# Top-k attention and a GELU layer on one core: reciprocals of the softmax sums made by POOL as a power, and eight more odd items transposed by DVE and DRAM

## The chip, the core and the metric

The program runs on one core of a Trainium2 chip. A core has five engines, each with a queue of its own that runs in the order in which the program was written: PE (TensorE: matmuls and transposes into PSUM), DVE (VectorE), ACT (ScalarE), POOL (GpSimd) and SP (SyncE, which here issues nearly all DMAs). They wait for each other through semaphores. Work that one queue holds up behind a wait stays held up, however ready it is.

The metric is the device time of one execution in microseconds (us); lower is better. The kernel before takes 1462.1 us, the median of three runs that lie between 1461.39 and 1462.64 us.

## The reference

Two blocks follow each other. The first is attention that keeps the 32 largest scores of each row:

```python
B, H, S, D = 8, 8, 576, 64
scores = (1 / sqrt(D)) * q @ k.transpose(0, 1, 3, 2)          # B, H, 576, 576
kth    = the 32nd largest of each row
scores = where(scores >= kth, scores, -1e9) - max of the row
attn   = exp(scores)
attn   = attn / (attn.sum(-1, keepdims=True) + 1e-09)
x      = (attn @ v).transpose(0, 2, 1, 3).reshape(B * S, H * D)   # 4608 x 512
```

The second is a layer with an exact GELU, `out = gelu(x @ w_in) @ w_out`, with `w_in` 512 x 2048 and `w_out` 2048 x 512. Everything is float32.

## The kernel before

**Items.** Heads are taken in pairs. An item is 128 rows of the scores of one pair: a tile `s` of 128 partitions by 2 x 576 scores (one row of each of the two heads in a partition). Each head has 576 = 4 x 128 + 64 rows. For each batch there are 16 items of full row blocks (4 pairs x 4 blocks, two neighbouring blocks of a pair after each other) and 2 items that hold the 64 remaining rows of two pairs each. That makes 18 items a batch and 144 in all. Two batches, 36 items, are one ring of the buffer of x, and the pattern repeats with that period: an item's *number in the period* is its index modulo 36. Numbers 16 to 19 are the items of remaining rows; apart from those, two neighbouring numbers (even, odd) share one product with v.

**Slots.** The main loop runs over slots n. In slot n the engines work on different items:

- PE multiplies q and k for items ahead (L408, L423: `s_ps`, and L373: `t_ps`, the last keys); from slot 14 on an even slot does it for two items, n+2 and n+3. ACT copies the scores to `s` (L416, L381).
- DVE runs `top_k(n)`: rounds of MAX8 and MATCH_REPLACE8 (L513, L516) that find the 32nd largest. Most items are "paired": `larger` (L446, DVE) makes the elementwise maximum of the two halves of each row, `sum_up` (L477) and `smaller` (L485) on POOL make the minimum, so that the first two rounds read half the elements.
- POOL makes the threshold of item n (`threshold`, L527 and L528). ACT selects and exponentiates item n-1 (L547, L559); the exponential also sums the row into `den`.
- POOL adds 1e-9 to `den` of item n-1 (`add_small`, L540), DVE takes the reciprocal (`inverse`, L534, in `last()` at the end of `top_k(n)`), and POOL multiplies the item by it (`normalise`, L582).
- Item n-2 has to be transposed, since the product with v contracts over the keys. There are two ways. *By PE:* `transposes` gives 1 + 8 PE transposes of 128 x 128 into PSUM (L666, L680), and ACT copies the result to `pt` (L669, L695). *Squared:* DVE transposes 32 x 32 squares in place (`square_p`, L614, in the middle of `top_k(n)`), SP writes the item to DRAM with four DMAs (`write_p`, L624, at the end of slot n), and a slot later SP reads it back in the wanted order with four DMAs (`read_p`, L634). For a squared item PE and ACT do neither the transposes nor the copies.
- PE multiplies `pt` by v (`attend`, L751, L762). This is done once for an even and an odd item together: 20 matmul records. `pt` has one buffer, so that the read of the next even item waits for this product.
- PE fills the rest of the slot with pieces of the GELU layer (`mlp`; L820 first matrix, L976 and L974 second one, with a seven-product scheme). `room_in(n)` says how many pieces a slot gets. What is left after the last item is done at the end.

**Which items are squared.** `squared(i)`: from item 27 on, every even item but number 12, the items of remaining rows but number 17, and the odd items that `moved(i)` names, those of 36 to 135 whose number is in `LATER = (3, 13, 25, 31)`. The product of a moved odd item is done in slot i+4, not i+3, in the middle of that slot (`mid`, `mids`). In such a slot `read_p(n - 3)` is issued only behind that product, followed by loads of v that were held back (`issue_soon`); `bare(n)` in `room_in` moves two GELU pieces between the neighbouring slots to make up for it.

**SP's queue.** The DMAs of one slot stand in this order: `read_p(n-3)` (where no product is pending), loads of q and k that follow the DVE transposes of the slot (L130), in a `mid` slot `read_p(n-3)` here, then held loads of v (L140, L144), `write_p(n-2)`, and stores of the output (L891).

Of the kernel before, what the change touches and what calls it, by code (L numbers as in the profile page):

```python
# [14 lines left out]
def kernel(  # L15
# [19 lines left out]
    nc = tc.nc  # L35
    f32, i32, u32 = mybir.dt.float32, mybir.dt.int32, mybir.dt.uint32
    bf16, i16, u16 = mybir.dt.bfloat16, mybir.dt.int16, mybir.dt.uint16
    AF = mybir.ActivationFunctionType
    ALU = mybir.AluOpType

    B, H, S, D = q.shape
    P = 128
# [19 lines left out]
    const = ctx.enter_context(tc.tile_pool(name="const", bufs=1))  # L62
# [47 lines left out]
    def flush():  # L110
        held[0] = False
        while late_issues:
            late_issues.pop(0)()
        late_issues.extend(later)
        later.clear()
# [61 lines left out]
    DIAGS = START - 1  # L177
    SINGLE = range(18, 28)
    words = {}
    bounds = const.tile([P, 2], f32, name="bounds")  # L180
    low, high = bounds[:, 0:1], bounds[:, 1:2]
    nc.gpsimd.memset(low, -EXP0 * 2.0**20)
    nc.gpsimd.memset(high, EXP0 * 2.0**-40)

# [71 lines left out]
    for b in range(B):  # L258
# [4 lines left out]
        last = [(b * NP + p, NM) for p in range(0, NP, 2)]  # L263
# [8 lines left out]
    N = len(items)  # L272
# [4 lines left out]
    few = [False]  # L277
# [55 lines left out]
    S_of, stat_of = {}, {}  # L333
# [98 lines left out]
    def paired(i):  # L432

        return PAIRED <= i < N and i not in SINGLE

    def halves_of(i):
        s = S_of[i].rearrange("p (e h n) -> p e h n", e=2, h=2)
        return s[:, :, 0], s[:, :, 1]

    have_larger = set()  # L440

    def larger(i):

        if paired(i) and i not in have_larger:
            have_larger.add(i)
            nc.vector.tensor_tensor(lists_for(i)[:, :, 0], *halves_of(i), op=ALU.max)  # L446

    def into_of(i):

        if i < 2 and i not in into_lists:  # L450
            into_lists[i] = work.tile([P, 2, 2, HS], f32, tag="pt", bufs=1, name="into")
        return into_lists.get(i, lists_of[i])
# [13 lines left out]
    def lists_for(i):  # L466

        if i not in lists_of:
            lists_of[i] = work.tile([P, 2, 2, HS], f32, tag="lists", name="lists")
        return lists_of[i]  # L470
# [10 lines left out]
    def smaller(i):  # L481

        if paired(i):
            both, top = lists_of[i][:, :, 1].bitcast(i32), lists_of[i][:, :, 0].bitcast(i32)
            nc.gpsimd.tensor_tensor(into_of(i)[:, :, 1].bitcast(i32), both, top, op=ALU.subtract)  # L485

    def top_k(i, last, middle):


        stat_of[i] = st = {  # L490
            "first": work.tile([P, 2, 8], f32, tag="first", name="first"),
        }
        stat = work.tile([P, 4, 2], f32, tag="stat", name="stat")
        st.update((n, stat[:, x]) for x, n in enumerate(("neg", "bias", "den", "rden")))
        top = work.tile([P, 2, 16], f32, tag="top", bufs=1, name="top")
        into = [st["first"]] + [
            top[:, :, 8:16] if r == TOPK // 8 - 1 else top[:, :, 0:8] for r in range(1, TOPK // 8)
        ]
        if paired(i):
            t = lists_of[i]  # L500
            u = into_of(i)
            both = u.rearrange("p e h n -> p e (h n)")
            rounds = [(t[:, :, 0], u[:, :, 0]), (u[:, :, 0], u[:, :, 0])]
            rounds = [(*(rounds[r] if 16 * r < TOPK else (both, both)), x) for r, x in enumerate(into)]
        else:
            s = S_of[i].rearrange("p (e n) -> p e n", e=2)
            t = work.tile([P, 2, S], f32, tag="lists", name="rest")
            rounds = [(s if r == 0 else t, t, x) for r, x in enumerate(into)]
        for r, (src, dst, x) in enumerate(rounds):
            if 16 * r == TOPK:  # L510
                middle()
            for e in range(2):
                nc.vector.max(x[:, e], src[:, e])  # L513
            if r < len(rounds) - 1:
                for e in range(2):
                    nc.vector.match_replace(dst[:, e], x[:, e], src[:, e], LOWEST)  # L516
            if r == len(rounds) - 1:
                last()

        st["kth"] = top[:, :, 15]  # L520

    def threshold(i):

        if i < 0 or i >= N:
            return
        st = stat_of[i]
        nc.gpsimd.tensor_scalar(st["neg"], st["kth"], -1.0, None, op0=ALU.mult)  # L527
        nc.gpsimd.tensor_tensor(st["bias"], st["kth"], st["first"][:, :, 0], op=ALU.subtract)  # L528

    def inverse(i):  # L530
        if i < 0 or i >= N:
            return
        st = stat_of[i]
        nc.vector.reciprocal(st["rden"], st["den"])  # L534

    def add_small(i):
        if i < 0 or i >= N:
            return
        st = stat_of[i]
        nc.gpsimd.tensor_scalar(st["den"], st["den"], 1e-9, None, op0=ALU.add)  # L540

    def select(i, e):

        if i < 0 or i >= N:
            return
        st, s = stat_of[i], row(i, e)
        nc.scalar.activation(s, s, func=AF.Prelu, bias=st["neg"][:, e : e + 1], scale=1.0, alpha=STEEP)  # L547
        selected.add((i, e))
# [37 lines left out]
    def squared(i):  # L586

        if not SINGLE.stop - 2 < i < N - 2:
            return False
        if items[i][1] == NM:  # L590
            return i % RINGS != RINGS // 2 - 1
        return moved(i) or (i % 2 == 0 and i % RINGS != 12)

    LATER = (3, 13, 25, 31)

    def moved(i):

        return RINGS <= i < N - 8 and i % RINGS in LATER

# [10 lines left out]
    def square_p(i):  # L610

        if squared(i):
            s = S_of[i]
            nc.vector.transpose(s, s)  # L614

    def write_p(i):

        if squared(i):
            turned[i] = d = dram.tile([SQ, NJ + NM, P // SQ, P], f32, tag="turned", name="turned")
            s = S_of.pop(i).rearrange("p (x j) -> p x j", j=SQ)  # L620
            d = d.rearrange("i c k n -> i (c k) n")
            for a in range(P // SQ):
                rows = slice(a * SQ, (a + 1) * SQ)
                nc.sync.dma_start(out=d[:, :, rows], in_=s[rows])  # L624
# [498 lines left out]
    def mlp(n):  # L1123
        for _ in range(n):
            if done[0] >= len(pieces) or pieces[done[0]][0] > ready[0] or left[0] == 0:
                return
            pieces[done[0]][1]()
            done[0] += 1
            left[0] -= 1
            if eager[0]:  # L1130
                run_gelus()
                run_small(9)
# [72 lines left out]
    for n in range(ahead):  # L1205
# [27 lines left out]
        if n > 0:  # L1233
            larger(n + 1)
# [58 lines left out]
        if few[0]:  # L1293
            room = ODD if n % 2 else 0
            if mid and (mid[0] in starts_next or mid[0] % RINGS == LATER[0]):
                mlp(1)
# [34 lines left out]
            softmax(n - 1, 1)  # L1331
        if n > 0:
            smaller(n + 1)
        add_small(n - 1)
        for piece in tr[-1:] + prep:
            piece(None)
            mlp(1)
# [5 lines left out]
        mlp(left[0])  # L1343
        run_gelus()
        if n < N:
            def last():
                if few[0]:
                    larger(n + 2)
                inverse(n - 1)

            top_k(n, last, lambda: square_p(n - 2))
            write_p(n - 2)
            flush()
            if n == 0:
                larger(1)
        else:
            inverse(n - 1)
        threshold(n)
        if n == 0:
            smaller(1)  # L1360
# [60 lines left out]
```

## Time and profile before

| | |
|---|---|
| median of 3 runs | 1462.1 us |
| the profiled execution's own time | 1461.3 us |
| its span, first to last instruction | 1459.5 us |
| granted TensorE clock | 1.00 |
| busy in the span: PE, DVE, ACT, POOL | 1442.6, 1329.6, 1056.4, 1128.4 us |
| last top-k ends, GELU pieces alone follow | about 1375 us |
| items transposed by DVE and DRAM | 68 of 144 |

Busy time is the time in which an engine had an instruction in work; the start of a matmul record to the start of the next is the pace of PE. In the groups, the columns are the line, the engine, the operation, the output and inputs with their shapes and the count; behind the first bar stand the busy time in us and the mean length of one in ns, behind the second the idle time of the engine just before them and what ended most of it. In a timeline the columns are the start in us, the length in us and the instructions, equal neighbours merged with their count. SP's DMA rows show the issue, and not the transfer.

### The profile page before, as it was taken

How to read it: one execution, taken by the hardware profiler on the slowest of the kernel's cores; microseconds unless marked ns; L12 is line 12 of the kernel's file. 1: busy time of each engine (PE TensorE's matmuls, PEld its weight loads, DVE VectorE, ACT ScalarE, POOL GpSimd, SP SyncE). 2: the span in 40 equal slices, each digit the busy share in tenths (PEclk: the TensorE clock that was granted, in tenths of full speed). 3: DMA queues.
4: the chain of work that ended last, by engine and by line, in shares of the span. 5: the costliest groups of instructions: out<-in, count | busy, mean ns of one | idle time of the engine just before them, and what ended most of it. 6: DMA issues, size and time to landing. Idle time of an engine off the chain costs nothing.

```text
span 1459.5 us, 26550 instructions
## 1 busy us (share of the span) xinstructions
PE 1442.6 (99%) x8621; PEld 1123.9 (77%) x8621; DVE 1329.6 (91%) x3339; ACT 1056.4 (72%) x1883; POOL 1128.4 (77%) x1290
## 2 busy tenths in 40 slices
PE   8999999999999999999999999999999999999999
PEld 6776678877777777787777778787777777787887
DVE  7999999999999999999999999999999999999601
ACT  7999977777777777767777777777676767677620
POOL 6877657877798878878888878887788887878632
PEclk9999999999999999999999999999999999999999
DMA  7524310045454446456554365456554444543200
GB/s 196 150 87 126 84 48 1 9 98 104 90 113 89 87 87 142 82 113 128 111 99 96 65 117 116 90 112 127 117 102 106 90 80 84 127 98 85 53 15 15
DMA packets 591819, 136.49 MB, mean 94 GB/s; under 512 B 504352, under 2 KB 583232, under 8 KB 591680
## 3 DMA queue, kind: packets, MB, share of 16 engines
q1 hardware_dynamic: 590416, 134.37, 43.5%
q8 instruction: 68, 1.11, 0.3%
q14 instruction: 71, 0.58, 0.1%
q10 hardware_dynamic: 1200, 0.39, 0.1%
q0 software_dynamic: 64, 0.03, 0.0%
HBM read 85.19 MB, written 49.55 MB: 92 GB/s over the span
## 4 chain that ended last, share of the span: by engine, by line
PE 44%; POOL 11%; DVE 7%; issue 3%; ACT 3%; DMA 1%; SPq 0%; DVEq 0%; POOLq 0%; ACTq 0%
PE h_ps L820 17%; PE y_ps L976 11%; PE o L751 5%; PE s_ps L408 3%; POOL s L582 3%; DVE top L513 3%; DVE lists L516 2%; POOL lists L485 2%; POOL lists L477 2%; PE seven L974 2%; PE tp L680 2%; PE y_ps L938 2%; PE y_ps L941 1%; DMA turned<-s 1%; DVE s L614 1%
## 5 line engine op out<-in xcount | busy, mean ns | idle before, releaser
L820 PE MATMUL h_ps<-xT,w_in_sb 128*128 128x256 f32 (+1 forms) x2560 | 533.0, 361 | 0.0
L820 PEld LDWEIGHTS h_ps<-xT,w_in_sb 128*128 128x128 f32 x2560 | 438.9, 191 | 69.2 <-issue 10.9
L513 DVE MAX8 top<-lists 128x8 f32<-128x576 f32 (+1 forms) x792 | 475.9, 641 | 0.0
L547 ACT ACTIVATE s<-s,stat 128x576 f32<-128x576 f32 x288 | 219.2, 786 | 123.0 <-POOL stat L527 122.9
L516 DVE MATCH_REPLACE8 lists<-top,lists 128x288 f32<-128x288 f32 (+1 forms) x528 | 308.0, 589 | 0.0
L582 POOL TENSOR_TENSOR s<-s,stat 128x1152 f32<-128x1152 f32 x135 | 284.8, 2109 | 10.1 <-DVE stat L534 5.3
L559 ACT ACTIVATE s<-s,stat 128x576 f32<-128x576 f32 x288 | 225.2, 787 | 7.6
L485 POOL TENSOR_TENSOR lists<-lists 128x576 int32<-128x576 int32 x132 | 186.6, 1413 | 3.1
L477 POOL TENSOR_TENSOR lists<-s 128x576 int32<-128x576 int32 x133 | 188.2, 1415 | 0.0
L540 POOL TENSOR_SCALAR stat<-stat 128x2 f32<-128x2 f32 x144 | 44.4, 309 | 163.0 <-ACT s L559 156.1
L751 PE MATMUL o<-pt,raw_v 128*64 128x256 f32 x1280 | 152.9, 384 | 1.0 <-ACT pt L685 0.4
L416 ACT ACTIVATE s<-s_ps 128x1024 f32<-128x1024 f32 x127 | 126.4, 1046 | 35.2 <-PE s_ps L408 35.0
L751 PEld LDWEIGHTS o<-pt,raw_v 128*64 128x64 f32 x1280 | 86.8, 136 | 80.9 <-issue 38.1
L976 PE MATMUL y_ps<-w_out_sb,sum 128*128 128x256 f32 x472 | 140.4, 379 | 0.0
L408 PE MATMUL s_ps<-kt,qm 64*128 64x512 f32 x512 | 131.2, 621 | 1.1 <-ACT s L414 0.8
L836 ACT ACTIVATE g<-h_ps 128x512 f32<-128x512 f32 x144 | 78.2, 595 | 66.6 <-PE h_ps L820 66.0
L446 DVE TENSOR_TENSOR lists<-s 128x576 f32<-128x576 f32 x133 | 106.2, 799 | 17.8 <-ACT s L381 5.8
L976 PE MATMUL y_ps<-w_out_sb,g 128*128 128x256 f32 x480 | 116.4, 382 | 0.0
L516 DVE MATCH_REPLACE8 lists<-first,lists 128x288 f32<-128x288 f32 x264 | 114.4, 439 | 0.0
L513 DVE MAX8 first<-lists 128x8 f32<-128x288 f32 x268 | 105.8, 434 | 0.0
L976 PEld LDWEIGHTS y_ps<-w_out_sb,g 128*128 128x128 f32 x480 | 90.4, 190 | 15.0 <-issue 3.1
L976 PEld LDWEIGHTS y_ps<-w_out_sb,sum 128*128 128x128 f32 x472 | 89.8, 190 | 12.1
(162 smaller groups left out, 2359.0 us busy)
## 6 DMA issues: line engine op xcount, KB each, us to landing
turned<-s SPq DMA_DIRECT2D x272, 144.0 KB, 3.6
pt<-turned SPq DMA_DIRECT2D x272, 144.0 KB, 3.2
raw_v<-in_v_dram SPq DMA_DIRECT2D x64, 128.0 KB, 2.5
raw_q<-in_q_dram SPq DMA_DIRECT2D x112, 72.0 KB, 2.3
raw_k<-in_k_dram SPq DMA_DIRECT2D x112, 72.0 KB, 2.4
out_dram<-y SPq DMA_DIRECT2D x30, 256.0 KB, 3.1
w_out_sb<-in_moe_w_in_dram SPq DMA_DIRECT2D x14, 511.8 KB, 4.9
w_out_sb<-in_moe_w_out_dram SPq DMA_DIRECT2D x10, 511.8 KB, 4.1
```

The source lines that it names most:

```text
L408: nc.tensor.matmul(s_ps[:, e], lhsT=q_t[rows, :], rhs=kt[rows, main_keys(pair)], start=True, stop=True)
L416: nc.scalar.activation(spread(s, S + TL, SM), s_ps, func=AF.Copy, scale=scale)
L477: nc.gpsimd.tensor_tensor(t[:, :, 1].bitcast(i32), a.bitcast(i32), b.bitcast(i32), op=ALU.add)
L485: nc.gpsimd.tensor_tensor(into_of(i)[:, :, 1].bitcast(i32), both, top, op=ALU.subtract)
L513: nc.vector.max(x[:, e], src[:, e])
L516: nc.vector.match_replace(dst[:, e], x[:, e], src[:, e], LOWEST)
L547: nc.scalar.activation(s, s, func=AF.Prelu, bias=st["neg"][:, e : e + 1], scale=1.0, alpha=STEEP)
L559: nc.scalar.activation(s, s, func=AF.Exp, bias=st["bias"][:, e : e + 1], scale=1.0, accum_out=st["den"][:, e : e + 1],)
L582: nc.gpsimd.tensor_tensor(s, s, wide, op=ALU.mult)
L751: nc.tensor.matmul(o[e * D : (e + 1) * D, 0:n], lhsT=vt[:, j, e, :], rhs=pt[:, e * NJ + j if j < NM else NM, :], start=(j == 0), stop=(j = ...
L820: nc.tensor.matmul(h_tile(u)[:, i, :], lhsT=w_in_sb[:, ko, f * P : (f + 1) * P], rhs=xT[:, ko, c0 : c0 + n], start=(ko == 0), stop=(ko == ...
L976: nc.tensor.matmul(acc[names][:, k], lhsT=lhsT, rhs=rhs, start=(j == 0 and k == 0), stop=(j == FT // 2 - 1 and k == 1),)
```

## The change

Two things are changed. The reciprocal of `den` is no longer made by DVE: POOL does it right behind its addition of 1e-9, as `den` to the power of -1, with the exponent in a third column of `bounds`. The hook at the end of `top_k` goes away with it, so that `larger(n + 2)` is written at the start of slot n+1 and not at the end of slot n. And `LATER` has three more numbers, 5, 23 and 33. In the range that `moved` allows these are the items 41, 77, 113, 59, 95, 131, 69 and 105: they are transposed by DVE and DRAM, and their product with v comes a slot later.

```diff
-    bounds = const.tile([P, 2], f32, name="bounds")
+    bounds = const.tile([P, 3], f32, name="bounds")
+    minus = bounds[:, 2:3]
...
+    nc.gpsimd.memset(minus, -1.0)
...
-    def top_k(i, last, middle):
+    def top_k(i, middle):
...
-            if r == len(rounds) - 1:
-                last()
...
     def inverse(i):
...
-        nc.vector.reciprocal(st["rden"], st["den"])
-
-    def add_small(i):
...
         nc.gpsimd.tensor_scalar(st["den"], st["den"], 1e-9, None, op0=ALU.add)
+        nc.gpsimd.tensor_tensor(
+            st["rden"], st["den"],
+            bass.AP(tensor=minus.tensor, offset=minus.offset, ap=[list(minus.ap[0]), [0, 2]]),
+            op=ALU.pow,
+        )
...
-    LATER = (3, 13, 25, 31)
+    LATER = (3, 5, 13, 23, 25, 31, 33)
...
-        add_small(n - 1)
+        inverse(n - 1)
...
         if n < N:
-            def last():
-                if few[0]:
-                    larger(n + 2)
-                inverse(n - 1)
-
-            top_k(n, last, lambda: square_p(n - 2))
+            top_k(n, lambda: square_p(n - 2))
...
-        else:
-            inverse(n - 1)
```

`larger` loses the set that kept it from running twice for an item. In the order of the engines' instructions the change takes 144 reciprocals from DVE and gives it 8 square transposes; POOL gets 144 powers; PE loses 8 x (1 + 8) transposes and ACT 8 x 2 copies from PSUM; SP gets 8 x (4 + 4) DMAs. Three of the pairwise maxima change places with a neighbour on DVE.

More of the change, by code (lines that the diff above doesn't have):

```diff
@@ L438, in halves_of @@
         return s[:, :, 0], s[:, :, 1]
-    have_larger = set()
     def larger(i):
-        if paired(i) and i not in have_larger:
-            have_larger.add(i)
+        if paired(i):
             nc.vector.tensor_tensor(lists_for(i)[:, :, 0], *halves_of(i), op=ALU.max)
@@ L533, in inverse @@
         st = stat_of[i]
-        nc.vector.reciprocal(st["rden"], st["den"])
-    def add_small(i):
[L537 to L540, printed above, removed]
+        nc.gpsimd.tensor_scalar(st["den"], st["den"], 1e-9, None, op0=ALU.add)
+        nc.gpsimd.tensor_tensor(
[3 more added lines that the diff above has]
+        )
     def select(i, e):
```

## The prediction

> **What bounds the kernel now.** I read the busy line of the page, the stages of the span, the timelines of PE and SP, and the waits. In a stage, the columns are its length, then busy time of PE, PE's weight loads, DVE, ACT and POOL, the clock, and the DMA share.
>
> ```profile
> PE 1442.6 (99%) x8621; PEld 1123.9 (77%) x8621; DVE 1329.6 (91%) x3339; ACT 1056.4 (72%) x1883; POOL 1128.4 (77%) x1290
> ...
> 0.00:93.70 93.70, 83.58 (x632) 66.96 (x632) 84.84 (x233) 83.91 (x144) 70.11 (x79) 1.00 0.56 160
> ...
> 516.50:858.50 342.00, 341.36 (x2018) 265.94 (x2016) 332.96 (x840) 249.09 (x451) 283.54 (x323) 1.00 0.52 105
> ...
> 1375.30:1459.50 84.20, 80.36 (x402) 68.66 (x399) 5.07 (x13) 18.20 (x39) 28.06 (x39) 0.99 0.04 13
> ```
>
> The second of these stages is one whole period of 36 items: PE lacks 0.6 us of 342, DVE 9. When the top-k is over, PE has 84 us of GELU pieces left. So what counts is PE's work plus each time PE stands still. That a busy PE is at its pace is seen from start to start, here around the product of items 104 and 105 with v (numbers 32 and 33):
>
> ```profile
> 1033.65 0.27 PE L666 MATMUL tp_t<-ident,s 128*128 128x128 f32 x1
> 1033.76 0.60 PE L976 MATMUL y_ps<-w_sum,sum 128*128 128x256 f32 x2
> ...
> 1034.63 1.04 PE L680 MATMUL tp<-ident,s 128*128 128x128 f32 x8
> 1035.50 0.60 PE L976 MATMUL y_ps<-w_sum,g 128*128 128x256 f32 x2
> ...
> 1044.46 4.48 PE L820 MATMUL h_ps<-xT,w_in_sb 128*128 128x256 f32 x20
> 1048.78 1.03 PE L974 MATMUL seven<-w_sum,g 128*128 128x256 f32 x4
> 1049.65 1.89 PE L976 MATMUL y_ps<-w_out_sb,g 128*128 128x256 f32 x8
> ```
>
> 20 records in 4.32 us and 4 in 0.87 are 0.216 us each on two different lines: PE runs without a pause.
>
> **The change, part by part.** *PE, 8 items less.* The rows above give one item's transposes: 0.11 us (1033.65 to 1033.76) and 0.87 us (1034.63 to 1035.50), 0.98 together, on the path. 8 x 0.98 = 7.9 us less.
>
> *ACT* loses 8 times the two copies out of PSUM. It is busy for 249 us of 342 and its place is not where the end is set: nothing.
>
> *DVE and POOL.*
>
> ```profile
> L534 DVE RECIPROCAL stat<-stat 128x2 f32<-128x2 f32 x144 | 22.7, 158 | 31.1 <-POOL stat L540 27.8
> ...
> L614 DVE STREAM_TRANSPOSE s<-s 128x1152 f32<-128x1152 f32 x68 | 92.8, 1365 | 0.0
> ...
> L528 POOL TENSOR_TENSOR stat<-top,first 128x2 f32<-128x2 f32 x144 | 55.9, 388 | 0.0
> ...
> L582 POOL TENSOR_TENSOR s<-s,stat 128x1152 f32<-128x1152 f32 x135 | 284.8, 2109 | 10.1 <-DVE stat L534 5.3
> ...
> ACT s L547 <- POOL stat L527: 122.9, 45, 6.2
> ...
> 1028.32 2.11 POOL L582 TENSOR_TENSOR s<-s,stat 128x1152 f32<-128x1152 f32 x1
> ```
>
> DVE gets 36 x 0.158 = 5.7 us a period back and 3 x 1.365 = 4.1 to do, besides losing the wait for POOL's addition in front of the reciprocal. It already keeps up with PE, so a gain there ends in a wait for the next scores, or for `normalise` in front of the square transpose: 0 us on the path. Only in the first ten slots, where PE has fillers and not work, could it count, 0 to 1.6 us (10 x 0.158); ACT (83.9 of 93.7 us, first stage) is as busy there as DVE (84.8), so I take 0. `larger` stays where it was on DVE but for three neighbours: 0.
>
> The price of a power on POOL is in no row. The nearest is L528, as small and of the same form without the power, 0.39 us; the far end is L582, 2.1 us, the longest that POOL does per item. I take 0.4. It stands in POOL's queue ahead of `threshold(n)`, for which ACT waits (122.9 us), of `normalise` and of `sum_up`. POOL has 342 - 283.5 = 58.5 us free in a period, 1.62 us an item, and `normalise` of item 105 ends at 1030.43, 3.2 us ahead of the transposes that need it (1033.65): at 0.4 us the cost is 0. If the cover is gone, from about 1.6 us on, each further tenth costs 13 us over 133 items.
>
> The Trainium skill, "GPSIMD Engine Reference", section 2.1, Instruction dispatch, says that the first call of a freshly loaded kernel pays some 6 us for loading code, without an instruction in the profile. No run shows yet whether the power is such a call; by that page the sum would be up to 6 us higher, once.
>
> *SP, 64 DMAs more.* This is the term that I think decides. SP's rows around items 102 to 106 (W = L624 writes to DRAM, R = L634 reads back, four DMAs each), and the four products with v of that stretch:
>
> ```profile
> 1016.35 3.26 SPq L624 DMA_DIRECT2D turned<-s  x4
> 1023.74 2.54 SPq L634 DMA_DIRECT2D pt<-turned  x4
> 1026.37 3.38 SPq L624 DMA_DIRECT2D turned<-s  x4
> 1029.85 3.02 SPq L130 DMA_DIRECT2D raw_k<-in_k_dram  x4
> 1033.04 2.54 SPq L634 DMA_DIRECT2D pt<-turned  x4
> 1035.62 0.61 SPq L140 DMA_DIRECT2D raw_v<-in_v_dram  x1
> ...
> 1037.48 0.51 SPq L144 DMA_DIRECT2D raw_v<-in_v_dram  x1
> 1038.09 2.15 SPq L130 DMA_DIRECT2D raw_q<-in_q_dram  x4
> 1042.37 4.07 SPq L624 DMA_DIRECT2D turned<-s  x4
> ...
> DMA to landing us min/median/max: 2.7/3.2/4.5
> ...
> SPq L634 <- DMA turned<-s: 116.4, 81, 4.2
> ...
> 774.41 3.33 SPq L624 DMA_DIRECT2D turned<-s  x4
> 780.59 2.54 SPq L634 DMA_DIRECT2D pt<-turned  x4
> 783.17 2.23 SPq L130 DMA_DIRECT2D raw_k<-in_k_dram  x4
> ...
> 1002.01 2.38 PE L751 MATMUL o<-pt,raw_v 128*64 128x256 f32 x20
> 1029.29 2.38 PE L751 MATMUL o<-pt,raw_v 128*64 128x256 f32 x20 [0.34 <-issue]
> 1039.24 2.38 PE L751 MATMUL o<-pt,raw_v 128*64 128x256 f32 x20
> 1057.18 2.38 PE L751 MATMUL o<-pt,raw_v 128*64 128x256 f32 x20
> ```
>
> The row with 3.2 is the landing of a read (L634). A squared item costs SP a W of 3.3 us, then the landing of that write before its R may start: 1019.61 to 1023.74, 4.1 us, and at a quiet place 777.74 to 780.59, 2.9 us; then an R of 2.54, whose last DMA, issued 0.6 before the end, lands 2.6 after it. Two squared items in a row thus cost 8.7 to 9.9 us of SP each, about a slot, and loads of q, k and v come on top. Today the run of squared neighbours ends after three: R of item 103 lands at 1023.74 + 2.54 + 2.6 = 1028.9, and PE takes it at 1029.29. There is 0.4 us to spare, and that is before number 33 joins.
>
> With it, in the order of the changed program, SP does behind the R at 1033.04: the loads of v (to 1038.0), W of 105 (to 1041.4), the landing (1044.3 to 1045.5), R of 105 (to 1046.8 or 1048.0; landed 1049.4 to 1050.6), the load of q (2.2), W of 106 (to 1052.4 or 1053.6), the landing (2.9 to 4.1), R of 106 (to 1057.8 or 1060.2; landed 1060.4 to 1062.8).
>
> PE wants them earlier. From the product at 1029.29 to that at 1057.18 are 27.89 us, less 0.98 of transposes 26.9. From a moved product to the next are 9.95 us now (1029.29 to 1039.24), and PE's order has one GELU piece of four records (0.86) less there afterwards: 9.1. So the product of 104 and 105 falls due at 1029.29 + 17.8 = 1047.1 and the next at 1056.2. PE stands 2.3 to 3.5 us at the first, and at the second the delay adds up to 4.2 to 6.6. PE's queue is in order, so this is lost. Items 69 and 105 both lie so: 8.4 to 13.2 us, and I take 11.
>
> Numbers 5 and 23 have the same chain without loads of q and v inside. From a moved product's end, R (2.54), W (3.4), landing (2.9), R (2.54) and its landing (2.6) are 14.0 us, against 17.8 - 2.3 = 15.5 until the next moved product: it fits. The even item behind (numbers 6 and 26) has a load of k in front of its R (as at 783.17) and may be up to 0.5 us late: 6 times 0 to 0.5, I take 1.
>
> *Sum*: 1461.3 (the profiled execution; span 1459.5 and 1.8 around it) - 7.9 + 11 + 1 = 1465.4. It ran 0.8 us below the median, so 1466.2: **1466 us**, where about 0.2% (2.9 us) is what a measurement of this kernel can tell from no change.
>
> **The rivals.** *SP is in time, and PE's saving stands* (the other side). Place: the reads of numbers 33 and 34. If the runs of squares start earlier against PE, because DVE no longer waits for POOL, or if writes land in 2.9 us and the loads of q or v slip elsewhere, the products find their data. It decides from about 4 us gained in SP's chain of 28. For it: DVE wins 27.8 us of waits. Against it: the chain starts with a DVE square that stands behind scores which PE makes, and from there SP has no idle time but landings. 1461.3 - 7.9 + 0.8 = 1454 us, and 1452.6 with the first slots.
>
> *The power is expensive.* POOL becomes the bound above 1.62 us an item: at 2.1 us (2.11 - 1.62) x 133 = 65 us, 1527 us. For it: no row shows a power, and POOL runs its operations at 2.1 us for 1152 elements already. Against it: two elements a partition is as little as L528 has.
>
> *DVE sets the pace, and not PE.* Then 22.7 + 27.8 us less and 8 x 1.365 = 10.9 more give 39.6 us less, 1422 us. Against it: PE's starts lie 0.216 us apart without a gap. The Trainium skill, "Perfetto Trace Analysis", Identifying the Most-Contended Engine, calls matmul busy time a bad measure for PE and takes the busy share of weight loads and the other engines' occupancy. By that rule DVE (91%) would be the bound before PE (77%), and this case would follow; the distances of PE's starts contradict it here.
>
> **How the numbers follow.** SP's chain holds PE up: 0.53, from 1461.3 - 7.9 + 8.4 + 0.8 = 1462.6 to 1461.3 - 7.9 + 13.2 + 3 + 0.8 = 1470.4, of which a quarter lies below 1465.0. SP in time: 0.28, 1452 to 1456 and a little above. The power expensive: 0.16. DVE the pace: 0.03. The range takes the first two with some of the power's lower prices: 1452 to 1476; the likeliest case alone has 1462 to 1471. Faster 0.26 + 0.03, so about 0.28; within 0.2%: 0.14 + 0.03, 0.17; slower 0.38 + 0.16 and rounding, 0.55.
>
> **What would show it.** PE's transposes fall by 72 records and L534 is gone. POOL has 144 rows of a power: near 0.4 us right, over 1.6 wrong. PE's rows have idle time in front of the products (L751) of items 69 and 105 and of the pairs after them, 2 to 4 us each, released by the read (L634); SP shows W, landing, R, q, W, landing, R without a pause there. The prediction is wrong if these products start with no gap, or if POOL's threshold comes late in every slot.

## The result, and the profile after

The changed kernel takes **1493.9 us** (median of 6 runs, 1491.6 to 1495.8) against 1461.9 us of the kernel before (1461.4 to 1462.6, 6 runs): a ratio of 1.0218, 95% interval 1.0205 to 1.0231. It is slower, as forecast, but by 32 us and not by 4; the predicted range ended at 1476 us. The profiled execution of the changed kernel has a span of 1491.5 us.

The busy line of the page, and the stages of the span (length, then busy time of PE, weight loads, DVE, ACT and POOL, then clock, DMA share and GB/s):

```profile
PE 1447.9 (97%) x8549; PEld 1118.1 (75%) x8549; DVE 1343.5 (90%) x3203; ACT 1049.1 (70%) x1867; POOL 1220.0 (82%) x1435
```

```profile
520.00:870.00 350.00, 339.53 (x1970) 261.50 (x1970) 335.31 (x799) 245.14 (x444) 303.04 (x355) 1.00 0.56 111
1406.80:1491.50 84.70, 80.38 (x402) 68.60 (x400) 4.73 (x11) 19.26 (x42) 29.50 (x41) 1.00 0.04 13
```

PE has its 72 records less, yet its row is no longer without gaps: in the second line of the stages 10.5 us of 350 are missing (0.6 of 342 before). The tail after the top-k is as long as before, 84.7 us, so what is lost is lost while the top-k runs. POOL has 92 us more. DVE, which by the prediction's rows gives up 22.7 us of reciprocals and gets 10.9 us of square transposes, is not busy for 11.8 us less but for 13.9 us more (1343.5 against 1329.6). The groups, of the changed kernel and then of the kernel before (busy us, mean ns, idle time in front and who ended it):

```profile
L543 ACT ACTIVATE s<-s,stat 128x576 f32<-128x576 f32 x288 | 218.3, 780 | 182.1 <-POOL stat L524 182.0
...
L484 POOL TENSOR_TENSOR lists<-lists 128x576 int32<-128x576 int32 x132 | 191.1, 1448 | 3.1
...
L445 DVE TENSOR_TENSOR lists<-s 128x576 f32<-128x576 f32 x133 | 122.1, 919 | 34.8 <-ACT s L383 23.5
...
L532 POOL TENSOR_TENSOR stat<-stat,bounds 128x2 f32<-128x2 f32 x144 | 107.2, 744 | 12.0
```

```profile
L446 DVE TENSOR_TENSOR lists<-s 128x576 f32<-128x576 f32 x133 | 106.2, 799 | 17.8 <-ACT s L381 5.8 <-DVE top L513 0.9
```

The power (L532) costs 744 ns and not 400. ACT's wait for POOL's threshold has grown from 122.9 to 182.0 us. DVE no longer stands at a reciprocal, but its `larger` has become longer, 919 for 799 ns, 15.9 us in all. The waits of PE say where its time goes (total, times, longest):

```profile
PE t_ps L375 <- ACT p L991: 10.4, 9, 1.6
PE tp_t L375 <- ACT p L991: 5.3, 10, 0.7
PE tp_t L656 <- POOL diag L569: 5.2, 4, 1.8
PE o L747 <- DMA pt<-turned: 4.6, 3, 2.5
PE o L747 <- DMA raw_q<-in_q_dram: 3.7, 1, 3.7
PE tp L676 <- ACT xT L752: 2.9, 3, 1.0
```

Before, the wait of these score matmuls for `p` (ACT's copy of the MLP's result out of PSUM) was 1.0 us. Three kinds of new waits stand here, then. Products (L747) wait for reads, as the prediction said. The score matmuls of the last keys (L375) wait until ACT has copied `p` and so freed the one PSUM bank that both use. And transposes (L676) wait until ACT has copied the result of a product with v into `xT` and so freed the PSUM tile that a moved product and these transposes share. The prediction had neither of the last two. The wait that is put down to a load of q belongs to the first kind: the product reads no q, and the read L630 in front of that load landed just before the product started (rows below).

### The profile page after: what moved, and what is told of

Same layout as the page of the kernel before. It is cut to its first block, busy times and chain, and to the rows that moved or that the text cites. A ratio compares the mean times of both kernels' runs of the same rounds, so it can differ in the third digit from the quotient of the medians.

```text
span 1491.5 us, 26747 instructions
## 1 busy us (share of the span) xinstructions
PE 1447.9 (97%) x8549; PEld 1118.1 (75%) x8549; DVE 1343.5 (90%) x3203; ACT 1049.1 (70%) x1867; POOL 1220.0 (82%) x1435
## 4 chain that ended last, share of the span: by engine, by line
PE 61%; POOL 16%; ACT 11%; DVE 5%; issue 4%; DMA 2%; SPq 1%; DVEq 0%; POOLq 0%; ACTq 0%
PE h_ps L816 22%; PE y_ps L972 12%; PE o L747 6%; PE s_ps L410 4%; POOL s L578 3%; PE tp L676 3%; POOL lists L484 2%; ACT s L543 2%; PE y_ps L934 2%; DVE top L512 2%; PE y_ps L916 2%; PE y_ps L937 2%; POOL lists L476 2%; PE seven L970 2%; ACT L832 2%
## 5 line engine op out<-in xcount | busy, mean ns | idle before, releaser
L816 PEld LDWEIGHTS h_ps<-xT,w_in_sb 128*128 128x128 f32 x2560 | 438.9, 190 | 67.6 <-issue 10.9
L543 ACT ACTIVATE s<-s,stat 128x576 f32<-128x576 f32 x288 | 218.3, 780 | 182.1 <-POOL stat L524 182.0
L484 POOL TENSOR_TENSOR lists<-lists 128x576 int32<-128x576 int32 x132 | 191.1, 1448 | 3.1
L531 POOL TENSOR_SCALAR stat<-stat 128x2 f32<-128x2 f32 x144 | 52.0, 361 | 152.2 <-ACT s L555 145.7
L747 PE MATMUL o<-pt,raw_v 128*64 128x256 f32 x1280 | 155.4, 389 | 8.9 <-DMA pt<-turned 4.6
L445 DVE TENSOR_TENSOR lists<-s 128x576 f32<-128x576 f32 x133 | 122.1, 919 | 34.8 <-ACT s L383 23.5
L747 PEld LDWEIGHTS o<-pt,raw_v 128*64 128x64 f32 x1280 | 88.5, 138 | 85.7 <-issue 42.4
L532 POOL TENSOR_TENSOR stat<-stat,bounds 128x2 f32<-128x2 f32 x144 | 107.2, 744 | 12.0
L610 DVE STREAM_TRANSPOSE s<-s 128x1152 f32<-128x1152 f32 x76 | 104.3, 1373 | 9.3 <-POOL s L578 9.3
```

The lines of the kernel that those rows point to most:

```text
L747: nc.tensor.matmul(o[e * D : (e + 1) * D, 0:n], lhsT=vt[:, j, e, :], rhs=pt[:, e * NJ + j if j < NM else NM, :], start=(j == 0), stop=(j = ...
L816: nc.tensor.matmul(h_tile(u)[:, i, :], lhsT=w_in_sb[:, ko, f * P : (f + 1) * P], rhs=xT[:, ko, c0 : c0 + n], start=(ko == 0), stop=(ko == ...
```

## The experiments

The diffs are shortened to the lines that matter. Four theories were held on the power and POOL. A: the power's place in POOL's queue, in front of the threshold, makes ACT late. B: the eight items and SP's queue carry the loss. C: the power costs by its sum, wherever it lies. D: POOL has no time left in some slots, whatever it has over the whole. For DVE, E: it has no time left there either; F is its rival: DVE has slack.

**The two halves of the change.**

```diff
 # e1_power_only: the changed kernel with
-    LATER = (3, 5, 13, 23, 25, 31, 33)
+    LATER = (3, 13, 25, 31)
 # e2_items_only: the kernel before with
-    LATER = (3, 13, 25, 31)
+    LATER = (3, 5, 13, 23, 25, 31, 33)
```

> The kernel after, with the list of moved odd items put back to the four of before: the power alone. Theory A (POOL's order: the power stands in POOL's queue between the addition, which waits for ACT's exponential, and the threshold, for which ACT waits; ACT then copies the MLP's result out of its only PSUM bank late and PE stands): of the +32 us, the PE saving is -7.9 and the two items of number 33 are +11, so the power alone is 32 + 7.9 - 11 = +29 us: 1491 us. Theory B (the eight items and SP's queue carry the loss): within 1460 to 1466 us.

> The kernel before with the seven moved numbers (3, 5, 13, 23, 25, 31, 33) and the reciprocal left on DVE: the items alone. Theory A: -7.9 us of transposes and about +11 us where PE stands in front of the products of items 69 and 105 and of the pairs behind them: 1461.9 - 7.9 + 11 = 1465 us. Theory B: near the kernel after, 1485 to 1494 us.

Measured: the power alone 1479.2 us, ratio 1.0122 (1.0107 to 1.0137), +17.8 us; the items alone 1478.1 us, 1.0111 (1.0094 to 1.0128), +16.7 us. Neither theory had both: each half costs about as much as the other, and their sum, 34.5, is near the 32 of the whole. PE's waits in the kernel with the items alone:

```profile
PE o L751 <- DMA pt<-turned: 5.0, 2, 2.8
PE tp L680 <- ACT xT L756: 3.7, 6, 1.0
PE o L751 <- DMA raw_q<-in_q_dram: 3.5, 1, 3.5
```

**Number 33 apart from 5 and 23.**

```diff
 # e3_without_33: the changed kernel with
+    LATER = (3, 5, 13, 23, 25, 31)
 # e7_items_without_33: the kernel before with the same list
```

> The kernel after without number 33 (six moved numbers). If SP's chain costs about 11 us at items 69 and 105, as PE's gaps there say, and PE sets the pace elsewhere: 1493.9 - 11 + 2 x 0.98 = 1485 us, and the gaps in front of these products are gone. If PE would have stood there anyway for ACT (the loss by POOL's order takes up the time): 1491 to 1495 us.

> The kernel before with moved numbers 3, 5, 13, 23, 25 and 31, the reciprocal on DVE: number 5 and 23 alone. By the difference that number 33 made beside the power (11.6 us): 1478.1 - 11.6 = 1466.5 us, slower than before though PE has 5.9 us less to do. If the loss by number 5 and 23 came only from SP being late after number 33, then 1461.4 - 5.9 + 1 = 1456.5 us, as predicted.

Measured: 1482.3 us (1.0147, 1.0132 to 1.0162), 11.6 us under the changed kernel, and 1468.2 us (1.0045, 1.0028 to 1.0062), 9.9 us under the kernel with all items. Two items of number 33 thus cost 9.9 to 11.6 us net, or 12 to 13.6 if PE's 2.0 us of saved transposes count in full. Numbers 5 and 23, six items, cost 6.5 us net although PE has 5.9 us less to do, and only 3.1 us beside the power (1482.3 against 1479.2). In the kernel with these six items and without the power a single product waits for a read, 0.7 us; SP isn't their price.

The rows of the changed kernel around item 105, SP (W = L620, R = L630) and the products:

```profile
1052.29 2.54 SPq L630 DMA_DIRECT2D pt<-turned  x4
...
1057.36 3.41 SPq L620 DMA_DIRECT2D turned<-s  x4
1064.49 2.56 SPq L630 DMA_DIRECT2D pt<-turned  x4
1067.09 2.22 SPq L130 DMA_DIRECT2D raw_q<-in_q_dram  x4
1069.42 3.38 SPq L620 DMA_DIRECT2D turned<-s  x4
1075.70 2.73 SPq L630 DMA_DIRECT2D pt<-turned  x4
```

```profile
715.51 3.85 PE L747 MATMUL o<-pt,raw_v 128*64 128x256 f32 x20 [2.52 <-DMA pt<-turned]
...
727.37 2.38 PE L747 MATMUL o<-pt,raw_v 128*64 128x256 f32 x20 [1.06 <-DMA pt<-turned]
...
1048.29 2.38 PE L747 MATMUL o<-pt,raw_v 128*64 128x256 f32 x20
...
1070.06 3.42 PE L747 MATMUL o<-pt,raw_v 128*64 128x256 f32 x20 [3.68 <-DMA raw_q<-in_q_dram]
...
1081.87 2.38 PE L747 MATMUL o<-pt,raw_v 128*64 128x256 f32 x20 [1.01 <-DMA pt<-turned]
```

This is the chain as it was forecast: v, W of 105 (to 1060.8), 3.7 us of landing, R, q, W of 106, 2.9 us of landing, R. R of 105 ends at 1067.05; with the 2.6 us that the prediction takes for its last landing that is 1069.65, and the product starts at 1070.06. PE stands 2.52 and 3.68 us at the first product, 1.06 and 1.01 at the next: 8.3 us. The products behind the long gaps then take 3.85 and 3.42 us for 2.38, 2.5 us more, because the granted clock falls, as this table of stretches shows (the column in front of the DMA share):

```profile
1066.30:1070.00 3.70, 0.08 (x1) 0.00 (x0) 3.60 (x12) 2.25 (x3) 3.68 (x5) 1.00 0.87 188
1070.00:1073.50 3.50, 3.44 (x21) 2.13 (x21) 3.50 (x10) 3.46 (x6) 2.71 (x2) 0.68 0.86 135
```

**The place in POOL's queue.**

```diff
 # e4_power_behind: the changed kernel, the power in a function of its own
         threshold(n)
+        power(n - 1)
         normalise(n - 1)
```

> The kernel after with one change of order on POOL: the power goes behind the threshold, in front of the normalisation; as many instructions, as long. Theory A: ACT has its threshold as early as before, so the 29 us are gone and the items' part stays: 1465 us, ACT's wait for the threshold back near 123 us. Theory C (the power's time on POOL as such, 107 us, or DVE slowed beside a busier POOL, whatever the place): still 1485 to 1495 us. In between, about 1475 us, if the normalisation, now later by 0.7 us, holds up PE's or DVE's transposes.

Measured: 1493.2 us (1.0219, 1.0204 to 1.0234), the changed kernel's time. Theory A falls: with the threshold in front of the power, PE still waits for ACT's copy of `p` (8.0 and 3.9 us), and ACT's wait for the threshold is 172.4 us. The rows of POOL show why the place doesn't matter. First the kernel before, then the kernel with the power alone, in the same slot (number 21):

```profile
560.00 0.73 POOL L1028 TENSOR_TENSOR y<-y 128x256 f32<-128x256 f32 x1
560.69 1.41 POOL L485 TENSOR_TENSOR lists<-lists 128x576 int32<-128x576 int32 x1
562.18 0.22 POOL L540 TENSOR_SCALAR stat<-stat 128x2 f32<-128x2 f32 x1
562.76 0.22 POOL L527 TENSOR_SCALAR stat<-top 128x2 f32<-128x2 f32 x1 [0.36 <-DVE top L513]
562.93 0.67 POOL L528 TENSOR_TENSOR stat<-top,first 128x2 f32<-128x2 f32 x1
563.71 2.11 POOL L582 TENSOR_TENSOR s<-s,stat 128x1152 f32<-128x1152 f32 x1
```

```profile
565.25 0.73 POOL L1024 TENSOR_TENSOR y<-y 128x256 f32<-128x256 f32 x1
565.94 1.41 POOL L484 TENSOR_TENSOR lists<-lists 128x576 int32<-128x576 int32 x1
567.44 0.74 POOL L531 TENSOR_SCALAR stat<-stat 128x2 f32<-128x2 f32 x1
568.26 0.72 POOL L532 TENSOR_TENSOR stat<-stat,bounds 128x2 f32<-128x2 f32 x1
568.95 0.22 POOL L524 TENSOR_SCALAR stat<-top 128x2 f32<-128x2 f32 x1
569.14 0.20 POOL L525 TENSOR_TENSOR stat<-top,first 128x2 f32<-128x2 f32 x1
569.29 2.11 POOL L578 TENSOR_TENSOR s<-s,stat 128x1152 f32<-128x1152 f32 x1
```

In the kernel before, POOL waits 0.36 us for DVE and for nothing else: it is just in time. With the power it has no pause, and the addition follows `smaller` (L484), not ACT: DVE's top-k has ended by 567.34, where its next `larger` starts, and the threshold comes 1.6 us later. In this slot, what is put into the queue pushes everything behind it. What follows from it, three slots on in the same kernel (POOL, then ACT, then PE):

```profile
596.93 0.71 POOL L532 TENSOR_TENSOR stat<-stat,bounds 128x2 f32<-128x2 f32 x1
597.62 0.23 POOL L524 TENSOR_SCALAR stat<-top 128x2 f32<-128x2 f32 x1
```

```profile
597.88 1.44 ACT L543 ACTIVATE s<-s,stat 128x576 f32<-128x576 f32 x2 [4.89 <-POOL stat L524]
599.34 1.28 ACT L832 ACT_TABLE_LOAD   x1
600.64 1.08 ACT L832 ACTIVATE g<-h_ps 128x512 f32<-128x512 f32 x2
601.61 0.38 ACT L991 COPY p<-seven 128x256 f32<-128x256 f32 x1
```

```profile
602.04 0.49 PE L375 MATMUL tp_t<-kt,qm 128*128 128x128 f32 x2 [1.58 <-ACT p L991]
```

ACT stands 4.89 us for the threshold, selects, runs a GELU, copies `p`, and PE has stood 1.58 us until that copy.

**Where in the period the power costs.** From the rows of POOL in the kernel before: between one addition and the next it stands still for only 0.24 us up to the addition of slots 5, 8, 14, 16, 18, 20, 21, 24 and 26 of each period, and for 2 to 5 us in most of the odd ones. The kernel with the power alone falls behind in slots 4 to 12 and 20 to 28 (by the starts of the first maxima of each slot). So the power was given to one part of the slots and the reciprocal to the rest:

```diff
 # e5_power_in_free_slots: the kernel before, and after POOL's addition
+        if by_pool(i):  # (i + 1) % 36 not in (4..8, 20..28)
+            nc.gpsimd.tensor_tensor(st["rden"], st["den"], minus, op=pow)
 # with  if not by_pool(i):  in front of DVE's reciprocal
 # e6_power_in_full_slots: the same with the opposite condition
```

> The kernel before (four moved numbers), with the power on POOL in 22 of 36 slots, and the reciprocal on DVE in the slots numbered 4 to 8 and 20 to 28, which hold the stretches where POOL stood still for only 0.24 us in most slots of the kernel before. Theory D (POOL has no time left in those slots, though it has 58 us a period over all; what is added there makes threshold, ACT and PE late): with the power in the free slots alone no loss, 1458 to 1462 us. Theory C (the 107 us of power cost by their sum, wherever they are): 22/36 of 17.8 us, 1472 us.

> The other half: the power on POOL in the slots numbered 4 to 8 and 20 to 28 alone, the reciprocal on DVE in the other 22. Theory D: the whole loss of the power alone, 1461.4 + 18 = 1479 us, or 1 to 3 us more, since what the kernel with the power everywhere wins back in its free slots is missing. Theory C: 14/36 of 17.8 us, 1468 us.

Measured: 1467.0 us (1.0035, 1.0022 to 1.0048), +5.3 us, and 1474.2 us (1.0084, 1.0069 to 1.0099), +12.5 us; together just the 17.8 of the power everywhere. (These two kernels keep the hook at the end of `top_k`, so of the 17.8 us nothing is left for its removal.) Both results lie about halfway between the forecasts of C and D. The 14 slots of 36 carry 70% of the loss, 0.22 us a power against 0.06 in the others: where the power stands does matter, as D says, and C's even spread is wrong. But the loss is not confined to those slots, as D had it. The other part holds three slots with 0.24 us, too (14, 16 and 18); that these make its 5.3 us was not tested.

**DVE's time in the slots of 5 and 23.**

```diff
 # e8_dve_twice: the kernel before, at the end of the top-k's rounds
+                if moved(i - 2, (5, 23)):
+                    for e in range(2):
+                        nc.vector.max(x[:, e], src[:, e])
```

> The kernel before, all its items as they were; in the six slots where a square of number 5 or 23 would stand, DVE does the last two maxima of the top-k a second time (2 x 0.64 = 1.28 us against 1.37 us of a square; the same values are written again). PE, SP and DMA have nothing more or less to do. Theory E (DVE, too, has no time left in these slots): 6 x 1.2 to 1.3 us, 1469 us. Rival F (DVE has slack, and number 5 and 23 lose by their reads through DRAM or by the new order of PE): no change, 1461 to 1463 us.

Measured: 1465.8 us (1.0028, 1.0017 to 1.0038), +4.1 us for 7.7 us of DVE. This lies between E and F: a good half of the added DVE time reaches the end. The starts of the first maxima show it slot by slot. The doubled maxima put slot 8 off by 1.1 us, of which 0.6 are given back by slot 12, and slot 26 by 1.3. In the kernel with numbers 5 and 23 the squares put slot 8 off by 1.1 us as well, and slot 26 by 1.3 to 1.6: PE's saved transposes win nothing there. The two kernels part in slot 11, by 0.86 us in each period. The rows of the kernel with 5 and 23 (PE, then ACT) show why:

```profile
437.90 2.38 PE L751 MATMUL o<-pt,raw_v 128*64 128x256 f32 x20
...
445.25 1.09 PE L680 MATMUL tp<-ident,s 128*128 128x128 f32 x8 [0.98 <-ACT xT L756]
```

```profile
444.85 0.35 ACT L756 COPY xT<-o 128x256 f32<-128x256 f32 x1
```

The moved product of number 5 writes the PSUM tile that the next transposes by PE need, and ACT's copy out of it starts 4.6 us behind the product's end. These waits are 1.0 us for each number 5 and 0.25 for each number 23, 3.7 in all; the group is in the list of the kernel with all items above, too. DVE's 4.1 us and 3 x 0.86 us in slot 11 make 6.7, against the 6.5 measured.

**Length against presence, and DVE's saving.**

```diff
 # e9_no_reciprocal: the kernel before, POOL's sum in the reciprocal's place
-        nc.vector.reciprocal(st["rden"], st["den"])
-        nc.gpsimd.tensor_scalar(st["den"], st["den"], 1e-9, None, op0=add)
+        nc.gpsimd.tensor_scalar(st["rden"], st["den"], 1e-9, None, op0=add)
 # e10_product_for_power: the kernel with the power alone
-            op=ALU.pow,
+            op=ALU.mult,
```

> The kernel before with no reciprocal at all: the normalisation multiplies by the sum itself, written by POOL's addition into the place of the reciprocal (so the result isn't a softmax). DVE loses 144 x 158 ns and its wait for POOL's addition; POOL, PE, SP have the same work. If DVE's saving lies off the path, as the prediction's 0 says: 1459 to 1462 us. If DVE is the pace in part of the slots, as the run with the maxima done twice says (4.1 us for 7.7 us of DVE's time): 1440 to 1455 us; the power's own cost on POOL is then the 17.8 us and this gain on top.

> The kernel with the power alone, with a multiplication by -1 in the power's place on POOL (same tiles, same shape; it leaves the reciprocal out). It is as small as the subtraction of the threshold, so about 0.2 to 0.39 us in place of 0.74. If the loss goes by the time that POOL is given in its full slots: between the kernel without a reciprocal and the kernel with the power, at 0.2/0.74 to 0.39/0.74 of the way, some 1462 to 1470 us. If one more instruction in POOL's queue and the wait on it make the loss, whatever its length: 1477 to 1480 us.

Measured: 1463.8 us (1.0013, 1.0003 to 1.0023) and 1466.4 us (1.0030, 1.0019 to 1.0042). Both kernels leave the reciprocal out. Even then the kernel isn't faster than before. That does not show that DVE's time is off the path, for DVE got none back. The page without the reciprocal has

```profile
PE 1444.4 (99%) x8621; PEld 1123.4 (77%) x8621; DVE 1334.7 (91%) x3195; ACT 1056.7 (72%) x1883; POOL 1123.6 (77%) x1290
...
L446 DVE TENSOR_TENSOR lists<-s 128x576 f32<-128x576 f32 x133 | 125.7, 946 | 26.2 <-ACT s L381 12.4 <-ACT s L392 2.8 <-DVE top L513 0.5
```

DVE is busy for 1334.7 us, against 1329.6 before. The rows of the 22.7 us of reciprocals had mostly overlapped their neighbours' (6.6 us of DVE's busy time were theirs alone), and `larger` has 19.5 us more. The product has 262 ns in the mean (37.7 us in all) and costs 2.6 us more than nothing; the power, 744 ns, 12.8 us more than the product for 69.5 us of POOL. So the length decides, at 0.18 us of time for 1 us of POOL between product and power. The longer `larger` is no rival for these 12.8 us: beside the product it takes 126.5 us, beside the power 122.3.

**A selective use, and less of POOL.**

```diff
 # e11_power_where_it_gains: as e5, with
+            return i < 24 or (i + 1) % 36 in (12..16, 29..32)
 # e12_no_addition: the kernel before without, e13_power_no_addition: the kernel with the power alone without
-        nc.gpsimd.tensor_scalar(st["den"], st["den"], 1e-9, None, op0=add)
```

> The kernel before with the power only where the kernel with it everywhere drew ahead of the kernel before (items 0 to 23, and the slots numbered 12 to 16 and 29 to 32), the reciprocal on DVE elsewhere. The gains seen there are 1.0 us in slots 12 to 16 of each of three periods, about 2 us before slot 20 and 0.3 us in slots 29 to 32: 1455 to 1458 us if they stay. If each is given back in the next full stretch: 1460 to 1464 us.

> The kernel before with POOL's addition of 1e-9 to the sum left out (the sum of the exponentials is at least 1 in float32, which the addition doesn't change); the reciprocal on DVE then waits for ACT alone. POOL has 45 us less (144 x 0.31). If POOL sets the pace in its full slots already in the kernel before: 1.5% of POOL's work less, at 12.8 us for 70 us (power against product) some 8 us less, 1454 us. If before is just under that point, and PE without a gap is the bound: 1460 to 1462 us.

> The kernel with the power alone, the addition of 1e-9 left out: POOL has 107 - 45 = 62 us more than in the kernel before, not 92. If the loss goes by POOL's time in its full slots: by the line from the product (38 us of POOL, +4.5) to the power (107 us, +17.8), +9 us: 1471 us. If it goes by the power's own time or by its place behind ACT's exponential, whatever else POOL is spared: 1478 to 1480 us.

Measured: 1463.0 us (1.0006, 0.9997 to 1.0016), no difference that can be told, so the gains are not there at the end. Without the addition 1458.2 us (0.9975, 0.9964 to 0.9985), 3.7 us **faster than the kernel before**: the one version here that beats both, by a quarter of a per cent. With the power and without the addition 1469.5 us (1.0052, 1.0039 to 1.0064), +7.6 where the line through product and power gave +9. Nothing about the power itself was changed in that kernel; POOL was spared another instruction (busy 1182.8 us, not 1219.8), and about 10 of the 17.8 us went. So it is POOL's whole time that counts, and not the power as such.

## Why the prediction was right in sign and wrong in size

- **PE, -7.9 us on the path.** The records went (8621 to 8549); the time was not won. Numbers 5 and 23 save PE 5.9 us and make the kernel 6.5 us slower. The step from "PE has no gap" to "PE's saving counts" failed: PE had no gap, but DVE had next to none (333 of 342 us busy), in stretches POOL had none, and PE's queue waits for PSUM that ACT frees behind them.
- **DVE, 0.** For the removed reciprocals the number was right, and the reason was not: DVE's gain was to end in waits, but DVE had no gain: without the reciprocals it is busy for 5.1 us more, `larger` above all. For the added squares the 0 was wrong: 1.28 us more on DVE in each of those six slots costs 4.1 us in all.
- **The power, 0.4 us a piece, cost 0.** The step that failed most. The price was mis-sized, 744 ns, and the bounds (0.39 to 2.1) held it. The cover was wrong, too: 1.62 us an item is POOL's free time averaged over a period, and in nine slots of 36 it is 0.24. So the cost set in far below the 1.6 us from which I let it decide: 2.6 us at 262 ns against no instruction in its place, and 17.8 us over the kernel before at 744. The slack of `normalise`, which I took from item 105, lay in a free stretch, and it was the threshold and `smaller` that became late.
- **The first call.** The first power takes 1.36 us (0.71 is the usual length) and starts 0.08 us behind the addition; no pause of 6 us stands there.
- **SP's chain, 11 us at items 69 and 105.** Right in place and mechanism; that the size fits is partly luck. The waits are 8.3 us, a little less than the 8.4 to 13.2 of the forecast: the first ones 2.52 and 3.68 (2.3 to 3.5 forecast), the second ones 1.06 and 1.01 (1.9 to 3.1 more forecast). Another 2.5 us come from the lower clock, which wasn't forecast. And DVE's squares of these items, taken as 0, put the next slot off by 1.26 us each in the kernel with the items alone, before any product waits. How much of the 9.9 to 11.6 us each of these makes was not taken apart.
- **Numbers 5 and 23 at SP, 1 us.** Right as far as SP goes (0.7 us of wait), but their price lay on DVE and on the PSUM tile that ACT frees.
- **The rivals.** "SP is in time" fell. "The power is expensive" was the nearest, with the wrong point: not an average of 1.62 us, but each slot's own. "DVE sets the pace" fell by its premise: it needed 39.6 us less on DVE, and DVE has 13.9 us more. That DVE's time does count in part, the doubled maxima show.

The sum by the runs: 17.8 (power) + 6.5 (numbers 5 and 23) + 9.9 (number 33) = 34.2 us, of which 32.0 is found in the whole; they overlap by 2.2. The overlap lies with numbers 5 and 23, which cost 3.1 us beside the power and not 6.5. Against the forecast the power has 17.8 more, 5 and 23 have 11.4 more (6.5 for -4.9), and number 33 has 1 to 3 more. The way from POOL through ACT to PE is shown in the rows of one slot and in the sums of the waits; what each slot's delay costs was not taken apart further.

## What to carry to other kernels

Look for cover slot by slot, not as a share of a period: an engine at 83% can have nothing left in a quarter of the slots, and its in-order queue carries a delay of 0.7 us through another engine to the one that sets the end. Where several engines are near the bound, less work on one of them need not be a gain (PE's 5.9 us here were none), and more on another can be a loss. Look, too, whether the time that is taken from an engine arrives: here DVE lost its reciprocals and was no less busy. Leaving out an instruction that the result doesn't need (the addition of 1e-9 to a sum that is at least 1) won 3.7 us here; the shift of work between engines won nothing.

## What the runs showed of the hardware

- **A DVE operation with two inputs beside one of POOL.** `larger` takes 0.76 us alone or beside POOL's operations of two elements, and much longer beside `smaller`; in the kernel with the power alone, DVE's rows are

```profile
567.34 0.76 DVE L445 TENSOR_TENSOR lists<-s 128x576 f32<-128x576 f32 x1
...
576.99 1.32 DVE L445 TENSOR_TENSOR lists<-s 128x576 f32<-128x576 f32 x1
```

and POOL's row beside the second of them

```profile
576.28 1.41 POOL L484 TENSOR_TENSOR lists<-lists 128x576 int32<-128x576 int32 x1
```

The first begins as POOL's `smaller` has ended (567.35, in the rows of POOL above), the second in the middle of it. Past 130 us of the changed kernel 31 of 118 have `smaller` as the POOL operation that they overlap most, at 1.29 us in the mean, against 2 in the kernel before. At 0.53 us each they make about the 16 us by which `larger` grew. It isn't the power's doing: without reciprocal and power `larger` grew by 19.5 us. That DVE comes to it earlier when it no longer waits for POOL's addition would explain this; it was not tested. The Trainium skill, "GPSIMD Engine Reference", section 8, Key points, says that GpSimd shares its SBUF interfaces with VectorE and contends with DVE instructions that have two SBUF inputs. The rows agree, and give the price.

- **The clock after a wait of 2.5 us.** Products behind gaps of 2.47 to 3.87 us took 3.42 to 4.54 us for 2.38 in the changed kernel and in the kernels with the items alone and with the power behind (six cases, clock 0.57 to 0.68 in those measured); behind gaps of 2.21 us and less they took 2.38. The Trainium skill, "TensorE: Matmul & The Clock Gate", section "Why this matters for your kernels", asks for no idle gap of more than about 3 us; here 2.5 were enough.
